# All twelve score products of a head pair ahead of its six masked minima, in a windowed attention with softplus FFN

## The chip, the core and the metric

The kernel runs on one core of one Trainium2 chip. The metric is the device time of one execution in microseconds (us). Five engines work beside each other, each with a queue of its own: TensorE (PE, with its weight loads shown as PEld), VectorE (DVE), ScalarE (ACT), GpSimd (POOL) and SyncE (SP, which issues the DMAs).

## The reference

A causal attention over a window of 64 positions, for 8 batches of 8 heads, sequences of 576 and a head size of 64, and behind it a dense layer pair with a softplus between them, on 4608 tokens of 512 numbers.

```
scores = scale * np.matmul(q, k.transpose(0, 1, 3, 2))
rel = pos[:, None] - pos[None, :]
mask = (rel >= 0) & (rel < window)
scores = np.where(mask, scores, -1000000000.0)
scores = scores - np.max(scores, axis=-1, keepdims=True)
attn = np.exp(scores)
attn = attn / (np.sum(attn, axis=-1, keepdims=True) + 1e-09)
x = np.matmul(attn, v)          # then (batch, position) x (head, channel)
h = x @ w_in
g = np.maximum(h, 0.0) + np.log1p(np.exp(-np.abs(h)))
out = g @ w_out
```

## The kernel before

**Tiles.** The 4608 tokens are cut into 12 blocks g of 384 tokens. A block's attention is done by head pairs hp (4 of them, two heads of 64 channels each), its FFN by 16 slices f of 128 hidden channels. So there are 48 head pairs and 192 FFN steps in all.

**Attention of one head pair** (`attention`, a generator whose `yield`s mark stages). The 384 query tokens are three query tiles j of 128, each of two chunks u of 64. A chunk needs the 128 keys of its own and the previous chunk. So a product of q and k (L219) is 64 queries by 128 keys, for one chunk and one head hh: twelve products per head pair, four per query tile. They are written to `sps`, one PSUM bank per head, in which the three query tiles stand beside each other in columns. VectorE's `tensor_tensor_reduce` (L226) then adds the mask to one query tile of one head, writes the scaled result to `st` and its minimum over the keys to `mn` (the scale is negative, so the minimum stands for the maximum). There are six of these per head pair. ScalarE takes six exponentials (L236), with the sums in `sm`; VectorE adds, inverts and multiplies (L244 to L246). For blocks 0 and 1 (`by_pe`) TensorE transposes the result (L254) and ScalarE copies it (L255); for the others it is split in two fp16 halves (ScalarE's cast `nat` L265, VectorE's rest L268), which DMAs transpose (L262) and VectorE adds (`pt`, L272). TensorE multiplies with v (L286), and the result is split into two parts x (ScalarE L291, VectorE L292), the FFN's input.

**FFN step** (g, f): `ffn_up` is twelve matmuls of 128x384 (L308) into one of two banks `ps_h`; ScalarE takes Abs, Exp and Ln (L312 to L314), VectorE completes softplus (L316), and g is split in two parts (L318 on ScalarE or VectorE, L319 on VectorE). `ffn_down` is nine matmuls of 128x512 (L329) into three banks `ps_o`; at a block's end they are copied (L348) and stored.

**Banks.** Scores and products with v take turns on three banks (`ps_a`, `bufs=3`). In block 0, odd head pairs use `ps_o` banks.

**What sets the order.** Every stage and FFN step is an event with a due time, two units of time per FFN step; events are sorted by it and emitted in that order. Up number n is due at 2n + 0.5 and down number n at 2n + 5.5, so a down comes three ups after its up has begun. From block 3 on, head pairs follow each other every 8 units (four FFN steps), and a head pair's stages are due at the offsets of `STG`: the loads at -13 and -5, the scores with their minima at 0, the exponentials at 3 and 4, the product with v at 16. That is when the scores of the head pair two further on are due, so in PE's queue L286 of one head pair stands directly in front of the scores of another. TensorE executes its work in exactly the emitted order (`MANUAL`); the other engines' order is made by a scheduler when the program is built. Each engine takes its own queue in order. The weights come as 64-bit words and are converted at the start (`load_w`: ScalarE L162 and L168, VectorE L163 to L165 and L169), beside the attention of blocks 0 and 1; their raw words share buffers with `st` of block 0.

Of the kernel before, what the change touches and what calls it, by code (L numbers as in the profile page):

```python
# [15 lines left out]
ALU = mybir.AluOpType  # L16

P = 128
TB = 384
NJ = TB // P  # L20
WIN = 64
BIG = 1.0e9
CH = 64
# [20 lines left out]
def window_attention_softplus_ffn(  # L44
# [34 lines left out]
    QSCALE = -1.0 / float(D) ** 0.5  # L79
# [22 lines left out]
    def spare(k, shape, dtype, name):  # L102
        return late.tile(shape, dtype, name=name, tag=f"spare{k}")
# [11 lines left out]
    heads = [slice(0, D), slice(D, P)]  # L115
    halves = [slice(0, CH), slice(CH, P)]
# [23 lines left out]
    mm, tp = nc.tensor.matmul, nc.tensor.transpose  # L140
# [34 lines left out]
    def attention(g, hp):  # L175
# [5 lines left out]
        def bank():  # L181
            if not odd0:
                return ps_a.tile([P, 512], F32, name="ps_a")

            taken_ps[0] += 1
            return ps_o.tile([P, 512], F32, name=f"ps_o{taken_ps[0] % NJ}")

        q_in = ld.tile([P, TB], F32, name="q_in", bufs=2)
        k_in = ld.tile([P, CH + TB], F32, name="k_in", bufs=2)
# [16 lines left out]
        if g == 0:  # L206

            st = spare(FIRST[hp], [P, 2, NJ, P], F32, "st0")
        else:
            st = att.tile([P, 2, NJ, P], F32, name="st", bufs=2)  # L210
        mn = att.tile([P, 2, NJ], F32, name="mn", bufs=2)
        sm = att.tile([P, 2 * NJ], F32, name="sm", bufs=2)
        sps = [bank() for _ in heads]
        for j in range(NJ):
            js = slice(j * P, (j + 1) * P)
            for u in range(2):
                a = 2 * j + u
                for hh in range(2):
                    mm(  # L219
                        sps[hh][halves[u], js], q_in[heads[hh], a * CH : (a + 1) * CH],  # L220
                        k_in[heads[hh], a * CH : (a + 2) * CH], start=True, stop=True,
                    )
            t = (t0 + j * P) % S
            m = mask_at[0] if t == 0 else mask_at[1] if t + P > S else mask
            for hh in range(2):
                nc.vector.tensor_tensor_reduce(  # L226
                    st[:, hh, j, :], sps[hh][:, js], m, QSCALE, 3.0e38, ALU.add, ALU.min, mn[:, hh, j : j + 1]
                )
            if by_pe or j == NJ - 1:
                yield  # L230
# [53 lines left out]
        for a, hh in itertools.product(range(2 * NJ), range(2)):  # L284
# [3 lines left out]
                start=(a == 0), stop=(a == 2 * NJ - 1), skip_group_check=True,  # L288
# [73 lines left out]
    for g in range(NB):  # L362
        for hp in range(NP):
            if g < 3:
                base = BASE[g] + PACE[g] * hp
            else:
                base = 2 * NF * (g - 1) + SHP * hp + SH
            stages = attention(g, hp)
            for at in STG if g >= 2 else STG0:
                events.append((base + at, lambda stages=stages: next(stages, None)))  # L370
# [59 lines left out]
```

## Time and profile before

| | |
|---|---|
| median of 3 runs | 1131.58 us (1131.5 to 1132.87) |
| profiled execution | 1132.96 us |
| span of its trace | 1131.2 us |
| mean granted TensorE clock | 0.957 |
| HBM traffic over the span | 59 GB/s |

The granted clock is the share of full speed that the chip's throttle gave TensorE. Its rows by stage are in the prediction. From about 100 us on, the kernel repeats one pattern: four FFN steps, then a product with v and the scores of a head pair. From 255 to 1010 us every such period has its scores; behind that none are left to do, and from 1047 us on only FFN steps. A matmul's record includes its way through the array, so records of queued matmuls overlap.

### The profile page before, as it was taken

How to read it: one execution, taken by the hardware profiler on the slowest of the kernel's cores; microseconds unless marked ns; L12 is line 12 of the kernel's file. 1: busy time of each engine (PE TensorE's matmuls, PEld its weight loads, DVE VectorE, ACT ScalarE, POOL GpSimd, SP SyncE). 2: the span in 40 equal slices, each digit the busy share in tenths (PEclk: the TensorE clock that was granted, in tenths of full speed). 3: DMA queues.
4: the chain of work that ended last, by engine and by line, in shares of the span. 5: the costliest groups of instructions: out<-in, count | busy, mean ns of one | idle time of the engine just before them, and what ended most of it. 6: DMA issues, size and time to landing. Idle time of an engine off the chain costs nothing.

```text
span 1131.2 us, 16632 instructions
## 1 busy us (share of the span) xinstructions
PE 1006.9 (89%) x6384; PEld 864.2 (76%) x6384; DVE 552.5 (49%) x1431; ACT 579.7 (51%) x1433; POOL 3.9 (0%) x23
## 2 busy tenths in 40 slices
PE   5449899998999899989998999899989999899998
PEld 3338787887887788878887788778877787788997
DVE  5895754545444444444445444544444544543332
ACT  5665666554445444455445544555455544544443
POOL 1000000000000000000000000000000000000000
PEclk9989999999999999998999999999998999999999
DMA  7652522312223223123112221222222311320000
GB/s 233 245 170 98 159 59 79 107 44 86 60 57 72 57 60 85 44 57 92 53 43 69 79 55 44 83 62 57 72 54 62 86 44 43 86 43 1 28 1 28
DMA packets 124048, 83.65 MB, mean 74 GB/s; under 512 B 67137, under 2 KB 116033, under 8 KB 122433
## 3 DMA queue, kind: packets, MB, share of 16 engines
q1 hardware_dynamic: 123968, 82.60, 25.5%
q8 instruction: 50, 0.82, 0.3%
q14 instruction: 30, 0.24, 0.1%
HBM read 56.62 MB, written 10.22 MB: 59 GB/s over the span
## 4 chain that ended last, share of the span: by engine, by line
PE 80%; DVE 11%; DMA 5%; ACT 2%; issue 1%; POOL 0%; POOLq 0%; ACTq 0%; SPq 0%; DVEq 0%
PE ps_h L308 38%; PE ps_o L329 34%; PE ps_a L219 5%; DMA raws<-in_w_words_dram 4%; PE ps_a L286 3%; DVE pt L272 3%; DVE st L226 2%; DVE g L319 2%; DVE x L292 1%; DMA raw<-in_w_words_dram 1%; ACT ws L162 1%; DVE w L169 0%; DVE ws L165 0%; DVE ws L164 0%; ACT st L236 0%
## 5 line engine op out<-in xcount | busy, mean ns | idle before, releaser
L308 PE MATMUL ps_h<-x,w 128*128 128x384 f32 x2304 | 476.0, 359 | 0.0
L308 PEld LDWEIGHTS ps_h<-x,w 128*128 128x128 f32 x2304 | 439.5, 203 | 20.8 <-issue 7.3
L329 PE MATMUL ps_o<-w,g 128*128 128x512 f32 x1728 | 437.0, 397 | 0.0
L329 PEld LDWEIGHTS ps_o<-w,g 128*128 128x128 f32 x1728 | 326.8, 191 | 61.4 <-DVE g L319 0.4
L316 DVE SCALAR_TENSOR_TENSOR u<-ps_h,u 128x384 f32<-128x384 f32 x192 | 106.9, 557 | 332.1 <-ACT u L314 332.1
L312 ACT ACTIVATE u<-ps_h 128x384 f32<-128x384 f32 x192 | 94.3, 491 | 312.7 <-PE ps_h L308 311.9
L219 PE MATMUL ps_a<-k_in,q_in 64*64 64x128 f32 x1104 | 93.3, 315 | 106.1 <-DVE mn L226 102.3
L219 PEld LDWEIGHTS ps_a<-k_in,q_in 64*64 64x64 f32 x1104 | 47.6, 140 | 144.2 <-DVE mn L226 134.5
L236 ACT ACTIVATE st<-st,mn 128x128 f32<-128x128 f32 x288 | 113.6, 395 | 74.5 <-DVE mn L226 74.3
L319 DVE TENSOR_TENSOR g<-u,g 128x384 fp32r<-128x384 f32 x192 | 106.9, 557 | 41.3 <-ACT g L318 35.5
L313 ACT ACTIVATE u<-u 128x384 f32<-128x384 f32 x192 | 100.9, 526 | 5.8
L314 ACT ACTIVATE u<-u 128x384 f32<-128x384 f32 x192 | 100.7, 525 | 5.4
L226 DVE CUSTOM_DVE_ANT_0 st<-ps_a,mask 128x128 f32<-128x128 f32 x276 | 71.3, 286 | 49.7 <-PE ps_a L219 49.4
L318 ACT CAST g<-u 128x384 fp32r<-128x384 f32 x112 | 57.3, 512 | 59.0 <-DVE u L316 57.7
L268 DVE TENSOR_TENSOR nat<-st,nat 128x768 f16<-128x768 f32 x40 | 38.3, 958 | 51.0 <-ACT nat L265 51.0
L286 PEld LDWEIGHTS ps_a<-pt,v_in 128*64 128x64 f32 x1104 | 38.9, 143 | 21.6 <-issue 15.9
L236 ACT ACTIVATION_READ_ACCUMULATOR st<-st,mn 128x1 f32 x288 | 53.8, 187 | 0.0
L265 ACT CAST nat<-st 128x768 f16<-128x768 f32 x40 | 33.1, 827 | 40.5 <-issue 40.5
L286 PE MATMUL ps_a<-pt,v_in 128*64 128x64 f32 x1104 | 46.0, 232 | 4.6 <-ACT pt L255 3.8
L272 DVE TENSOR_TENSOR pt<-tr 128x768 f32<-128x768 f16 x40 | 38.3, 958 | 23.0 <-PE ps_a L286 21.7
L246 DVE TENSOR_TENSOR st<-st,sm 128x768 f32<-128x768 f32 x48 | 46.0, 958 | 1.5
L318 DVE CAST g<-u 128x384 fp32r<-128x384 f32 x80 | 28.8, 360 | 5.7
(48 smaller groups left out, 277.2 us busy)
## 6 DMA issues: line engine op xcount, KB each, us to landing
v_in<-in_v_dram SPq DMA_DIRECT2D x44, 384.0 KB, 3.4
raws<-in_w_words_dram SPq DMA_DIRECT2D x12, 1024.0 KB, 5.6
k_in<-in_kT_dram SPq DMA_DIRECT2D x44, 224.0 KB, 2.7
q_in<-in_qT_dram SPq DMA_DIRECT2D x48, 192.0 KB, 2.4
out_dram<-raw SPq DMA_DIRECT2D x12, 512.0 KB, 3.0
raw<-in_w_words_dram SPq DMA_DIRECT2D x8, 512.0 KB, 3.7
out_dram<-raw SPq DMA_DIRECT2D x12, 256.0 KB, 4.1
v_in<-in_v_dram SPq DMA_DIRECT2D x4, 320.0 KB, 4.2
```

Of the source, the lines that this page charges most:

```text
L219: mm(sps[hh][halves[u], js], q_in[heads[hh], a * CH : (a + 1) * CH], k_in[heads[hh], a * CH : (a + 2) * CH], start=True, stop=True,)
L226: nc.vector.tensor_tensor_reduce(st[:, hh, j, :], sps[hh][:, js], m, QSCALE, 3.0e38, ALU.add, ALU.min, mn[:, hh, j : j + 1])
L236: nc.scalar.activation(sv[:, i, :], sv[:, i, :], AF.Exp, bias=mn[:, hh, j : j + 1], scale=-1.0, accum_out=sm[:, i : i + 1])
L286: mm(av[heads[hh], cs], v_in[:, a, heads[hh]], pt[:, hh, cs], start=(a == 0), stop=(a == 2 * NJ - 1), skip_group_check=True,)
L308: mm(hv, weight(0, a, f)[:, c * P : (c + 1) * P], x[b][c], start=(i_mm == 0), stop=(i_mm == 3 * NC - 1))
L312: nc.scalar.activation(u, hv, AF.Abs)
L313: nc.scalar.activation(u, u, AF.Exp, scale=-1.0)
L314: nc.scalar.activation(u, u, AF.Ln, bias=1.0)
L316: nc.vector.scalar_tensor_tensor(gf, hv, 0.0, u, ALU.max, ALU.add)
L318: (nc.scalar.copy if g < 2 or f % 2 else nc.vector.tensor_copy)(gt[0], gf)
L319: nc.vector.tensor_tensor(gt[1], gf, gt[0].bitcast(F32), ALU.subtract)
L329: mm(ops[g][j], gt[a][:, js], weight(1, b, f), start=(first and i == 0), stop=(last and i == 2),)
```

## The change

The four products of a query tile stood directly ahead of its two minima, tile by tile. Now one loop emits all twelve products, in the order as before (tile, chunk, head), and a second loop the six minima, also in the order as before. The stages' ends (`yield`) stand with the minima as before. Lines behind this place have numbers smaller by one in the changed kernel: L216 is the product there, L224 the minimum, L307 and L328 the FFN's matmuls.

```
+        for j, u, hh in itertools.product(range(NJ), range(2), range(2)):
+            a = 2 * j + u
+            mm(
+                sps[hh][halves[u], j * P : (j + 1) * P], q_in[heads[hh], a * CH : (a + 1) * CH],
+                k_in[heads[hh], a * CH : (a + 2) * CH], start=True, stop=True,
+            )
         for j in range(NJ):
-            js = slice(j * P, (j + 1) * P)
-            for u in range(2):
-                a = 2 * j + u
-                for hh in range(2):
-                    mm(
-                        sps[hh][halves[u], js], q_in[heads[hh], a * CH : (a + 1) * CH],
-                        k_in[heads[hh], a * CH : (a + 2) * CH], start=True, stop=True,
-                    )
             t = (t0 + j * P) % S
             m = mask_at[0] if t == 0 else mask_at[1] if t + P > S else mask
             for hh in range(2):
                 nc.vector.tensor_tensor_reduce(
-                    st[:, hh, j, :], sps[hh][:, js], m, QSCALE, 3.0e38, ALU.add, ALU.min, mn[:, hh, j : j + 1]
+                    st[:, hh, j, :], sps[hh][:, j * P : (j + 1) * P], m,
+                    QSCALE, 3.0e38, ALU.add, ALU.min, mn[:, hh, j : j + 1],
                 )
             if by_pe or j == NJ - 1:
                 yield
```

PE's queue has the same instructions in the same order. What differs there are the semaphores that they wait for. Before, at one head pair late in the steady stage (ps_a are the score banks, ps_h the next FFN step's; xN is the number of equal rows):

```order
L286 MATMUL ps_a<-pt,v_in 64x64 [waits DMAHW0_49,PE_49]
L286 MATMUL ps_a<-pt,v_in 64x64 x11
L219 MATMUL ps_a<-k_in,q_in 64x128 [waits DMAHW2_49,DMAHW1_49,PE_49]
L219 MATMUL ps_a<-k_in,q_in 64x128 [waits PE_49]
L219 MATMUL ps_a<-k_in,q_in 64x128 x2
L219 MATMUL ps_a<-k_in,q_in 64x128 [waits DVE_49] x2
L219 MATMUL ps_a<-k_in,q_in 64x128 x2
L219 MATMUL ps_a<-k_in,q_in 64x128 [waits DVE_49] x2
L219 MATMUL ps_a<-k_in,q_in 64x128 x2
L308 MATMUL ps_h<-x_0_0_6837,w_85 128x384
```

And the same place in the changed program:

```order
L285 MATMUL ps_a<-pt,v_in 64x64 [waits DMAHW0_49,PE_49]
L285 MATMUL ps_a<-pt,v_in 64x64 x11
L216 MATMUL ps_a<-k_in,q_in 64x128 [waits DMAHW2_49,DMAHW1_49,PE_49]
L216 MATMUL ps_a<-k_in,q_in 64x128 [waits PE_49]
L216 MATMUL ps_a<-k_in,q_in 64x128 x10
L307 MATMUL ps_h<-x_0_0_6837,w_85 128x384 [waits DVE_49]
```

The four products that waited for VectorE, two at the second and two at the third query tile, wait for nothing now; the FFN's first matmul behind them carries a wait for VectorE that the products had covered.

ScalarE's queue around the exponentials of one steady head pair, before:

```order
L291 ACTIVATE x_0_1_4563<-ps_a 128x384
L236 ACTIVATE st,sm<-st,mn 128x128 x6
L265 CAST nat<-st 128x768
L312 ACTIVATE u<-ps_h 128x384
L313 ACTIVATE u<-u 128x384
L314 ACTIVATE u<-u 128x384
```

And in the changed program:

```order
L290 ACTIVATE x_0_1_4563<-ps_a 128x384
L235 ACTIVATE st,sm<-st,mn 128x128 x6
L311 ACTIVATE u<-ps_h 128x384
L312 ACTIVATE u<-u 128x384
L313 ACTIVATE u<-u 128x384
L264 CAST nat<-st 128x768
```

The cast `nat` moved behind the three functions of the next FFN step. On VectorE, the same head pair's rows before:

```order
L272 TENSOR_TENSOR pt<-tr 128x768
L319 TENSOR_TENSOR g_4542<-u,g_4541 128x384
L226 ISA st,mn<-ps_a,mask_103 128x128
L226 ISA mn 128x1
L292 SCALAR_TENSOR_TENSOR x_0_1_4564<-ps_a,x_0_1_4563 128x384
L226 ISA st,mn<-ps_a,mask_103 128x128
```

And in the changed program:

```order
L271 TENSOR_TENSOR pt<-tr 128x768
L318 TENSOR_TENSOR g_4542<-u,g_4541 128x384
L291 SCALAR_TENSOR_TENSOR x_0_1_4564<-ps_a,x_0_1_4563 128x384
L224 ISA st,mn<-ps_a,mask_103 128x128
L224 ISA mn 128x1
L224 ISA st,mn<-ps_a,mask_103 128x128
```

The second part of x moved ahead of the first minimum; further down, the rest of `nat` (L268) moved from ahead of the next L316 to behind it and the cast of g (L318). In the first 100 us, conversions and minima change places on VectorE and ScalarE in many rows, and on SP's queue some loads of raw weights stand elsewhere among the loads of k and v. SP's queue is otherwise the same, but for one load of `part`.

## The prediction

> **What bounds the kernel now.** I read the page first (busy time by engine), then the waits, then TensorE's timeline around one head pair, then windows from one head pair to the next.
>
> ```profile
> PE 1006.9 (89%) x6384; PEld 864.2 (76%) x6384; DVE 552.5 (49%) x1431; ACT 579.7 (51%) x1433; POOL 3.9 (0%) x23
> ```
>
> ```profile
> PE ps_a L219 <- DVE mn L226: 102.3, 125, 4.7
> ```
>
> TensorE (PE) is busy 1006.9 of 1131.2 us; VectorE (DVE) and ScalarE (ACT) about half. Nearly all that PE lacks is one wait, 102.3 us: score products (L219) waiting for masked minima (L226). What it looks like, in rows of PE's timeline (start, duration, engine, line, operation, count, idle time before):
>
> ```profile
> 981.72 0.92 PE L286 MATMUL ps_a<-pt,v_in 128*64 128x64 f32 x24
> 982.57 0.45 PE L219 MATMUL ps_a<-k_in,q_in 64*64 64x128 f32 x8
> 984.38 0.43 PE L219 MATMUL ps_a<-k_in,q_in 64*64 64x128 f32 x2 [1.36 <-DVE mn L226]
> 985.05 0.44 PE L219 MATMUL ps_a<-k_in,q_in 64*64 64x128 f32 x6 [0.25 <-DVE mn L226]
> 985.89 0.65 PE L219 MATMUL ps_a<-k_in,q_in 64*64 64x128 f32 x8 [0.40 <-DVE mn L226]
> 986.48 3.91 PE L308 MATMUL ps_h<-x,w 128*128 128x384 f32 x12
> 990.23 2.26 PE L329 MATMUL ps_o<-w,g 128*128 128x512 f32 x9
> ...
> 142.84 4.16 PE L308 MATMUL ps_h<-x,w 128*128 128x384 f32 x12
> ...
> 1029.17 2.37 PE L308 MATMUL ps_h<-x,w 128*128 128x384 f32 x12
> ```
>
> Twelve products show as 24 records, eight for each query tile. From 982.57 to 986.48 they hold PE for 3.91 us, most of it waiting twice for minima of the tile before: both tiles stand in one PSUM bank. Then twelve L308 matmuls hold PE 3.75 us (986.48 to 990.23). Windows from one L286 to the next (length, busy time by engine; the number after POOL is PE's granted clock):
>
> ```profile
> 959.99:981.72 21.73, 19.73 (x133) 16.88 (x132) 10.93 (x30) 11.54 (x29) 0.00 (x0) 1.00 0.30 57
> 981.72:1005.03 23.31, 21.31 (x133) 18.45 (x132) 10.85 (x30) 11.35 (x29) 0.00 (x0) 0.93 0.28 68
> 1028.32:1046.12 17.80, 17.80 (x109) 15.88 (x108) 6.51 (x13) 7.69 (x15) 0.00 (x0) 1.00 0.00 1
> ...
> 254.55:1028.32 773.77, 705.82 (x4489) 608.13 (x4488) 358.54 (x971) 383.81 (x960) 0.00 (x0) 0.95 0.23 62
> ```
>
> The third window holds the same four FFN steps and the same L286, but no scores: 17.80 us with PE never idle. With scores it is 21.73 at clock 1.00, or 23.31 at 0.93: **the waits cost twice**, as idle time and, in many periods, as a slow clock behind them. The last row is the whole steady stage: 4488 weight loads at 132 a period are 34 periods. At 21.73 each they would take 738.8; the 35.0 us left over are about 22 periods of the slow kind (1.58 each).
>
> **The change part by part.** It adds and removes no instruction. PE's order is the same; what goes are the two waits inside each head pair's scores. The six minima wait for the last product of their bank, so nothing on PE stands between a head pair's first score and the L308 behind it.
>
> *Price of the scores alone.* The first eight above take 0.45 with a last matmul of about 0.27, so they start 0.18 apart, and the next eight could start at 0.21: three times that is 0.63. Below, the weight load of L308 shows a changeover.
>
> ```profile
> 508.68 3.56 PEld L308 LDWEIGHTS ps_h<-x,w 128*128 128x128 f32 x12 [0.17 <-issue]
> ```
>
> 0.63 + 0.17 = 0.80, my value: the scores stay queued behind L286 as the first eight are. The lower bound is 0.63; the upper is three times what the last eight take after a wait, 986.48 - 985.89 = 0.59, so 1.77.
>
> *Steady stage.* 34 x (17.80 + 0.80) = 632.4 in place of 773.77: **-141.4**, of which about 35 is clock.
>
> *The six head pairs before it* have no L286 beside their scores (first, second and the sum of six windows from first score to next step):
>
> ```profile
> 136.17:142.84 6.67, 1.95 (x26) 1.11 (x25) 6.34 (x18) 4.77 (x13) 0.00 (x0) 0.79 0.48 151
> 159.47:161.96 2.49, 1.69 (x25) 0.98 (x24) 1.14 (x9) 2.35 (x8) 0.00 (x0) 1.00 0.01 3
> sum 19.11, PE 10.38 PEld 6.04 DVE 13.74 ACT 15.44 POOL 0.00; mean PE 1.73 PEld 1.01 DVE 2.29 ACT 2.57 POOL 0.00
> ```
>
> 19.11 becomes 6 x 0.80 = 4.8: **-14.3**. The first is also followed by a slow L308 (4.16 in the timeline above, against 2.37 at 1029.17, where the clock is 1.00): **-1.8**.
>
> *The head, 0 to 100 us*, with eight head pairs and the weight conversion:
>
> ```profile
> 0.00:28.00 28.00, 15.64 (x148) 10.50 (x148) 14.76 (x60) 15.58 (x52) 3.94 (x23) 1.00 0.73 233
> 28.00:56.00 28.00, 13.32 (x118) 9.09 (x119) 24.38 (x57) 17.85 (x47) 0.00 (x0) 1.00 0.71 249
> 56.00:84.00 28.00, 13.59 (x121) 10.00 (x120) 27.27 (x59) 18.48 (x48) 0.00 (x0) 0.90 0.52 173
> 84.00:100.00 16.00, 14.26 (x100) 11.89 (x102) 9.80 (x20) 9.64 (x22) 0.00 (x0) 0.85 0.37 118
> ```
>
> Here DVE is the bound from 28 to 84 (51.65 of 56), so PE's waits there are mostly hidden: PE would only wait elsewhere. DVE's idle time from 28 to 100 is 10.6 us, the most there is to win. The scheduler also reorders conversions and minima here, and SP's loads of raws move past loads of v_in; the two dearest kinds of a conversion's DVE steps are
>
> ```profile
> L169 DVE TENSOR_TENSOR w<-ws,w 128x512 fp32r<-128x512 f32 x24 | 15.7, 681 | 0.3 <-ACT w L168 0.3
> L164 DVE SCALAR_TENSOR_TENSOR ws<-raws,ws 128x1024 uint32<-128x1024 uint32 x12 | 14.7, 1222 | 0.1
> ```
>
> two of each, some 3.8 us; two such conversions ahead of minima that end the head would cost 7.6. I take **-4**, between +7.6 and -10.6, nearer the gain, because PE's waits there hold back the transposes and products behind them, which ScalarE and DVE go on from.
>
> *What the moved DVE and ACT work does.* In the steady stage x (L292) goes ahead of the first minimum, and ACT's nat cast (L265) and DVE's L268 go behind the next u. Is anything late for PE's next steps? One period in order, with durations from rows (L313 taken as L314, L319 and x as L316, L246 and L268 as L272, which has as many elements):
>
> ```profile
> 504.89 0.96 DVE L272 TENSOR_TENSOR pt<-tr 128x768 f32<-128x768 f16 x1 [0.75 <-PE ps_a L286]
> ...
> 507.96 0.28 DVE L226 CUSTOM_DVE_ANT_0 st<-ps_a,mask 128x128 f32<-128x128 f32 x1
> 508.17 0.08 DVE L226 DVE_READ_ACCUMULATOR2_ANT mn<- 128x1 f32 x1
> ...
> L316 DVE SCALAR_TENSOR_TENSOR u<-ps_h,u 128x384 f32<-128x384 f32 x192 | 106.9, 557 | 332.1 <-ACT u L314 332.1
> L312 ACT ACTIVATE u<-ps_h 128x384 f32<-128x384 f32 x192 | 94.3, 491 | 312.7 <-PE ps_h L308 311.9
> L236 ACT ACTIVATE st<-st,mn 128x128 f32<-128x128 f32 x288 | 113.6, 395 | 74.5 <-DVE mn L226 74.3
> L314 ACT ACTIVATE u<-u 128x384 f32<-128x384 f32 x192 | 100.7, 525 | 5.4
> L265 ACT CAST nat<-st 128x768 f16<-128x768 f32 x40 | 33.1, 827 | 40.5 <-issue 40.5
> ```
>
> Let L286 start at 0. PE: scores 0.85 to 1.65, L308 to 3.9, L329 to 5.95, next L308 to 8.05, L329 to 10.15, third L308 from 10.15; it needs the first one's bank, and the L329 at 12.25 needs its g. DVE: pt 0.96 to 1.9, L319 to 2.4, x to 2.9, six minima at 0.21 (507.96 to 508.17) to 4.15. ACT: six exponentials from 3.2, 0.40 each, to 5.6, then L312 to L314, 1.6, to 7.2. DVE: L246 to 7.1, L316 to 7.75 (bank free, due 10.15), the cast to 8.1, L268 after ACT's nat (8.05) to 9.05, L319 to 9.6 (due 12.25). So the cover is 2.4 us: **0**, and each us beyond it would cost 34. The loads of a period (first window) of 11.5 (ACT) and 10.9 (DVE) fit in 18.6.
>
> **Sum.** The profiled execution took 1132.96 us (1.38 over the median, 1131.58): 1132.96 - 141.4 - 14.3 - 1.8 - 4 = **971.5**.
>
> **Rivals.**
>
> *The clock stays slow.* If the thin matmuls (L286 and scores, 1.65 us at a stretch) and not the idle time bring the clock down, the 35 us stay: 1006. For it: the pattern of fast and slow periods depends on where the stretch falls. Against: the 2.49 us window at 159.47, scores with idle time in it, ran at 1.00, as did L286 alone at 1028.32. The Trainium skill ("TensorE: Matmul & The Clock Gate", "Why this matters for your kernels") says that only idle gaps over about 3 us throttle the array. By that rule the slow L308 would have another cause, and the sum would be this rival's. The trace speaks against the rule: no gap here is over 1.36, yet L308 took 3.91.
>
> *The products come at the slow pace*, 1.77: 40 x 0.97 = 38.8 more, 1010. For it: pace after a wait. Against: no wait is left before them.
>
> *DVE and ACT become late* by 1 us beyond the 2.4 in each period: 1005; by 2, 1040. For it: in-order queues with a burst of exponentials. Against: the replay above.
>
> *Nothing happens*: a wait for minima stays for another reason, 1131. Against: PE's rows of the change hold none.
>
> *Slower*: PE without pauses is held to a lower clock in the steady stage. It decides below 971.5/1132.96 = 0.86; at 0.79, the lowest row above, 971.5/0.79 = 1230. Against:
>
> ```profile
> 100.00:136.00 36.00, 36.00 (x190) 32.62 (x186) 21.18 (x39) 22.27 (x45) 0.00 (x0) 1.00 0.38 122
> 1028.00:1131.00 103.00, 98.79 (x530) 88.28 (x528) 34.16 (x64) 42.12 (x82) 0.00 (x0) 0.99 0.04 16
> ```
>
> PE was busy 36.00 of 36 and 98.79 of 103 us at clocks of 1.00 and 0.99. The Trainium skill (same page, Part 1) has a limiter at 13/16 clock once three cores of a die run dense matmuls; one runs here, and no run here shows it.
>
> **How the numbers follow.** Forecast 0.80, clock stays slow 0.08, late engines 0.05, slow pace 0.03, nothing 0.02, slower 0.02. Anything beyond 0.2% of 1131.58, about 2.3 us, can be told from no change. Faster 0.96, same 0.02, slower 0.02. The range: down by the rest of the head (6.6) and of the scores (40 x 0.17 = 6.8) to 958; up to the slow pace, 1010, which takes in the clock's rival and the first us of the late engines.
>
> **What would show it.** Right: L219 without a wait for L226, 0.7 to 1 us from first score to next step, periods of 18.6, granted clock near 1.00 from 255 us on, the end of the head within 10 us of 100. Wrong: L308 groups of 3.7 us still behind scores (clock), PE waiting for L316 or L319 (late engines), or the head longer by more than 7.6.

## Result and profile after

The changed kernel takes **969.12 us** (median of 4 runs, 967.93 to 974.21) where the kernel before takes 1132.22 us beside it (4 runs, 1131.5 to 1133.0): a ratio of 0.857, 95% interval 0.854 to 0.860. The forecast was 971.5 us. The profiled execution is the slowest of the four, 974.21 us with a span of 972.4; the working below goes by it. In the changed kernel the scores are L216, the minima L224 (two lower than before), and the lines behind them one lower: L286 has become L285, and the two FFN products are L307 and L328.

The page's busy times and granted clock in 40 slices:

```profile
PE 923.3 (95%) x6384; PEld 814.9 (84%) x6384; DVE 539.0 (55%) x1431; ACT 564.5 (58%) x1433; POOL 3.9 (0%) x23
...
PEclk9568989999999999999999999999999999999999
```

The number of instructions on each engine is the same. TensorE's busy time fell by 83.6 us (1006.9 to 923.3) although it does the same matmuls. The larger part are the records of the products themselves, which overlap less when products wait in between:

```profile
L219 PE MATMUL ps_a<-k_in,q_in 64*64 64x128 f32 x1104 | 93.3, 315 | 106.1 <-DVE mn L226 102.3
...
L216 PE MATMUL ps_a<-k_in,q_in 64*64 64x128 f32 x1104 | 44.8, 297 | 3.8 <-DMA k_in<-in_kT_dram 3.8
```

These are 48.5 us. The FFN's matmuls, slow ones before among them, fell from 476.0 to 443.8 and from 437.0 to 433.5. The granted clock is at 90% or more from the seventh slice on. It is lower in the second to fourth slices, which lie in the head, and in the sixth (122 to 146 us). TensorE's waits, the longest first, have no row for scores that wait for minima, where before had 102.3 us in it. The first row, a wait in the head for ScalarE's copies of the transposed results, has grown from 3.8 us to 11.3:

```profile
PE ps_a L285 <- ACT pt L254: 11.3, 9, 3.7
...
PE ps_h L307 <- DVE u L315: 3.4, 1, 3.4
```

The timeline at one head pair of the steady stage (start, duration, line, operation, count), and at the one place behind the head where a new wait stands:

```profile
254.79 0.92 PE L285 MATMUL ps_a<-pt,v_in 128*64 128x64 f32 x24
255.64 0.89 PE L216 MATMUL ps_a<-k_in,q_in 64*64 64x128 f32 x24
256.45 2.38 PE L307 MATMUL ps_h<-x,w 128*128 128x384 f32 x12
258.67 2.26 PE L328 MATMUL ps_o<-w,g 128*128 128x512 f32 x9
...
140.36 4.21 PE L307 MATMUL ps_h<-x,w 128*128 128x384 f32 x12 [3.36 <-DVE u L315]
144.37 3.00 PE L328 MATMUL ps_o<-w,g 128*128 128x512 f32 x9
```

The twelve products are now one group of 24 records that hold TensorE for 0.81 us (255.64 to 256.45) where they held it for 3.91 at 982.57 before, and the L307 behind them takes 2.38 us, not the 3.91 of that place. At 140.36, once, the third L307 waits for VectorE and then runs slowly. Windows (length, busy time by engine, clock) over the head, one period, the whole steady stage and the period without scores:

```profile
0.00:28.00 28.00, 13.98 (x162) 11.01 (x162) 14.23 (x54) 14.28 (x47) 3.94 (x23) 0.85 0.75 238
28.00:56.00 28.00, 10.72 (x110) 8.04 (x110) 24.75 (x68) 19.57 (x57) 0.00 (x0) 0.50 0.75 260
...
236.12:254.79 18.67, 18.67 (x133) 16.56 (x133) 10.74 (x31) 10.69 (x28) 0.00 (x0) 1.00 0.36 109
236.12:869.59 633.47, 633.47 (x4490) 561.61 (x4489) 347.25 (x971) 370.77 (x960) 0.00 (x0) 1.00 0.29 76
869.59:887.38 17.79, 17.79 (x109) 15.87 (x108) 6.50 (x13) 7.69 (x15) 0.00 (x0) 1.00 0.00 1
```

In the steady stage TensorE is busy 633.47 of 633.47 us at clock 1.00; before, the same 34 periods took 773.77. By line, over these two windows, the difference of 140.3 is about 68 us of idle time in front of products, 37 in the products' own records (67.1 to 30.1) and 36 in the FFN's matmuls (344.8 to 311.5 and 309.2 to 306.6), which is the part of the slow clock. By stages, before against after:

| stage | before, us | after, us | difference | predicted |
|---|---|---|---|---|
| head, to the first two L307 groups in a row | 100.20 | 91.53 | -8.7 | -4 |
| from there to the steady stage, six head pairs | 154.35 | 144.59 | -9.8 | -16.1 |
| steady stage, 34 periods | 773.77 | 633.47 | -140.3 | -141.4 |
| sum, with the rest of the span (equal within 0.1) | | | -158.8 | -161.5 |

### The profile page after: what moved, and what is told of

It is laid out like the page before. It is cut to its first block, busy times and chain, and to the rows that moved or that the text cites. A ratio compares the mean times of both kernels' runs of the same rounds, so it can differ in the third digit from the quotient of the medians.

```text
span 972.4 us, 16615 instructions
## 1 busy us (share of the span) xinstructions
PE 923.3 (95%) x6384; PEld 814.9 (84%) x6384; DVE 539.0 (55%) x1431; ACT 564.5 (58%) x1433; POOL 3.9 (0%) x23
## 4 chain that ended last, share of the span: by engine, by line
PE 87%; DMA 6%; DVE 3%; ACT 3%; issue 0%; SPq 0%; ACTq 0%; DVEq 0%
PE ps_h L307 41%; PE ps_o L328 39%; PE ps_a L285 4%; DMA raws<-in_w_words_dram 4%; PE ps_a L216 3%; DMA raw<-in_w_words_dram 2%; ACT st L235 1%; ACT ws L162 1%; DVE w L169 1%; DVE ws L164 0%; DVE ws L165 0%; DMA part<-raw 0%; DVE st L245 0%; ACT wh L162 0%; DVE st L224 0%
## 5 line engine op out<-in xcount | busy, mean ns | idle before, releaser
L307 PE MATMUL ps_h<-x,w 128*128 128x384 f32 x2304 | 443.8, 341 | 3.4 <-DVE u L315 3.4
L328 PE MATMUL ps_o<-w,g 128*128 128x512 f32 x1728 | 433.5, 395 | 1.4 <-DVE g L318 1.4
L307 PEld LDWEIGHTS ps_h<-x,w 128*128 128x128 f32 x2304 | 409.1, 189 | 24.1 <-issue 6.9
L328 PEld LDWEIGHTS ps_o<-w,g 128*128 128x128 f32 x1728 | 322.2, 188 | 62.3 <-DVE g L318 2.0
L315 DVE SCALAR_TENSOR_TENSOR u<-ps_h,u 128x384 f32<-128x384 f32 x192 | 107.0, 557 | 253.4 <-ACT u L313 249.7
L235 ACT ACTIVATE st<-st,mn 128x128 f32<-128x128 f32 x288 | 111.9, 391 | 67.1 <-DVE mn L224 67.1
L318 DVE TENSOR_TENSOR g<-u,g 128x384 fp32r<-128x384 f32 x192 | 106.6, 555 | 38.7 <-ACT g L317 33.8
L312 ACT ACTIVATE u<-u 128x384 f32<-128x384 f32 x192 | 100.9, 526 | 5.8
L317 ACT CAST g<-u 128x384 fp32r<-128x384 f32 x112 | 57.4, 512 | 57.7 <-DVE u L315 56.6
L285 PEld LDWEIGHTS ps_a<-pt,v_in 128*64 128x64 f32 x1104 | 40.1, 146 | 34.1 <-issue 20.2
L224 DVE CUSTOM_DVE_ANT_0 st<-ps_a,mask 128x128 f32<-128x128 f32 x276 | 61.8, 286 | 9.6 <-PE ps_a L216 9.6
L285 PE MATMUL ps_a<-pt,v_in 128*64 128x64 f32 x1104 | 47.6, 236 | 16.8 <-ACT pt L254 11.3
L216 PE MATMUL ps_a<-k_in,q_in 64*64 64x128 f32 x1104 | 44.8, 297 | 3.8 <-DMA k_in<-in_kT_dram 3.8
L216 PEld LDWEIGHTS ps_a<-k_in,q_in 64*64 64x64 f32 x1104 | 32.7, 144 | 8.6 <-POOL mask L135 3.8
L243 DVE TENSOR_SCALAR sm<-sm 128x6 f32<-128x6 f32 x40 | 6.9, 172 | 54.4 <-ACT st L235 54.3
```

The source lines that it names most:

```text
L216: mm(sps[hh][halves[u], j * P : (j + 1) * P], q_in[heads[hh], a * CH : (a + 1) * CH], k_in[heads[hh], a * CH : (a + 2) * CH], start=True, ...
L224: nc.vector.tensor_tensor_reduce(st[:, hh, j, :], sps[hh][:, j * P : (j + 1) * P], m, QSCALE, 3.0e38, ALU.add, ALU.min, mn[:, hh, j : j + 1],)
L235: nc.scalar.activation(sv[:, i, :], sv[:, i, :], AF.Exp, bias=mn[:, hh, j : j + 1], scale=-1.0, accum_out=sm[:, i : i + 1])
L285: mm(av[heads[hh], cs], v_in[:, a, heads[hh]], pt[:, hh, cs], start=(a == 0), stop=(a == 2 * NJ - 1), skip_group_check=True,)
L307: mm(hv, weight(0, a, f)[:, c * P : (c + 1) * P], x[b][c], start=(i_mm == 0), stop=(i_mm == 3 * NC - 1))
L312: nc.scalar.activation(u, u, AF.Exp, scale=-1.0)
```

## The experiments

Seven new kernels, and the changed kernel once more. Each stands beside runs of the kernel before on its own chip (1131.7 to 1132.3 us). Theory A is the prediction's: the waits between the products cost their idle time and, through the clock, slow matmuls behind them. Its main rival was that the thin matmuls, and not the idle time, bring the clock down.

### Half of the change: steady stage alone, and head alone

A helper emits the four products of one tile, either all ahead or tile by tile; `by_pe` is true in blocks 0 and 1, the head. This is the edit for the steady stage alone; for the head alone the line reads `ahead = NJ if by_pe else 0`.

```diff
-        for j, u, hh in itertools.product(range(NJ), range(2), range(2)):
+        def products(j):
...
+        ahead = 0 if by_pe else NJ
+        for j in range(ahead):
+            products(j)
         for j in range(NJ):
...
+            if j >= ahead:
+                products(j)
```

Steady stage alone (blocks 2 and later):

> The change for blocks 2 to 11 alone (40 head pairs), blocks 0 and 1 as before. My theory: the terms are separate, so this keeps the steady stage (34 periods of 18.63 in place of 22.76, about 140 us) and the six head pairs ahead of it, and loses only the head's gain (8.7 us in the trace of the change: 100.20 against 91.53): 974 to 980 us, granted clock 1.00 in the steady stage. Rival: the head's gain is chance or comes back later as waits for weights: 967 to 971.

Head alone:

> The change for blocks 0 and 1 alone (8 head pairs), the 40 others as before. My theory: PE's waits in the head held back transposes and products, so the end of the head moves from 100.2 to about 91.5 us: 1121 to 1126 us. Rival: the head is bound by DVE and by the loads of weights, and nothing is won there: 1130 to 1133.

Measured: **980.07 us** for the steady stage alone (979.52 to 980.74, 4 runs; ratio 0.866, interval 0.864 to 0.867) and **1121.31 us** for the head alone (1117.56 to 1122.76, 4 runs; ratio 0.990, interval 0.987 to 0.992). The second lies in theory A's range, the first at its upper edge, 0.07 us beyond it and far from the rival's. So the change in the head is worth 10.9 us by the one (980.07 - 969.12; 8.9 against 971.16, the second set of runs of the changed kernel, further down) and 10.9 by the other (1132.16 - 1121.31), more than the 4 of the forecast, and the two halves add up within 2 us.

Where does the head's gain come from? VectorE is the bound there, and it loses both idle time and work. The sums of four windows over the head, first of before and then of after, and VectorE's rows of one step of the large weight conversions inside each head:

```profile
sum 100.20, PE 57.02 PEld 41.61 DVE 76.41 ACT 61.56 POOL 3.94; mean PE 14.25 PEld 10.40 DVE 19.10 ACT 15.39 POOL 0.98
L164 DVE SCALAR_TENSOR_TENSOR ws<-raws,ws 128x1024 uint32<-128x1024 uint32 x12 | 14.7, 1222 | 0.1
```

```profile
L164 DVE SCALAR_TENSOR_TENSOR ws<-raws,ws 128x1024 uint32<-128x1024 uint32 x11 | 13.4, 1222 | 0.1
```

Before, VectorE was busy 76.41 of 100.20 us of the head, idle 23.8. In the first 91.50 us of after it is busy 70.22 (14.23 + 24.75 above, and 22.32 + 8.92 in two more windows up to 91.50), idle 21.3. Of the 8.7 us, 2.5 are idle time that went and 6.2 are busy time. Most of that, 4.5, is one of the twelve large conversions, which now comes later (x12, x11): two steps of 1.22 us, two of 0.68 and one of 0.69. Another 0.6 is one step of the FFN that comes later too, and 1.2 are the minima: the same 48, whose records overlap more when they follow each other directly (12.0 to 10.8). Behind the head VectorE has slack for the conversion: it is busy 87.67 of the 144.59 us up to the steady stage. The prediction named the reordered conversions only as a risk.

The profiled execution of after is the slowest of its four, and its head is longer than in two other traces of the changed head. With the head alone and with the changed kernel again, the head ends at 89.49 and 88.40 us, and VectorE is idle for 18.4 and 17.4 us of it. So there 5.4 and 6.4 of the 10.7 and 11.8 us are idle time that went, about half.

In both kernels that change blocks 2 and later there is also the new wait. With the steady stage alone, where the head is as before, TensorE's timeline has it too (its lines are L314 for L307 and L322 for L315):

```profile
148.22 2.03 PE L314 MATMUL ps_h<-x,w 128*128 128x384 f32 x10 [3.15 <-DVE u L322]
```

So the wait does not come from the conversion that was put off in the head. (The row ends with its window, at 150 us. The whole group takes 2.38 us: behind this wait of 3.15 us nothing is slow.)

### What brings the clock down: thin matmuls five times over, without a gap

```diff
-        for j, u, hh in itertools.product(range(NJ), range(2), range(2)):
+        for _, j, u, hh in itertools.product(range(1 if by_pe else 5), range(NJ), range(2), range(2)):
```

> The change, with the twelve products of each head pair in blocks 2 to 11 made five times over (same results): PE has small matmuls for as long a stretch as before, about 4 us, and no idle time in it. Forty head pairs with 4 x 0.65 to 0.81 us more are 104 to 130 us. If idle time brings the clock down: 1073 to 1100 us at a granted clock of 1.00 in the steady stage. If the small matmuls do: about 35 us more, 1108 to 1135, and L307 groups of 3.7 us behind two periods in three.

Measured: **1076.12 us** (2 runs). The timeline of a steady period:

```profile
418.48 0.92 PE L285 MATMUL ps_a<-pt,v_in 128*64 128x64 f32 x24
419.32 3.51 PE L216 MATMUL ps_a<-k_in,q_in 64*64 64x128 f32 x120
422.76 2.37 PE L307 MATMUL ps_h<-x,w 128*128 128x384 f32 x12
```

4.28 us of thin matmuls at a stretch (418.48 to 422.76), and the L307 behind them takes 2.37 us, the full pace. The products cost 3.44 instead of 0.81; 40 times the difference is 105 us, and 969.12 + 105 = 1074. Between 250 and 960 us the granted clock is 1.00. The rival falls: thin matmuls without a gap do not bring the clock down.

### One gap in each period

One product is emitted again behind the six minima, into columns that the last of them read, so TensorE waits for them:

```diff
+            if not by_pe and j == NJ - 1:
+                mm(
+                    sps[1][halves[1], j * P : (j + 1) * P], q_in[heads[1], 5 * CH : 6 * CH],
+                    k_in[heads[1], 5 * CH : 7 * CH], start=True, stop=True,
+                )
```

> The change, with one more product (a repeat of the last one, same result) behind the six minima in blocks 2 to 11: it waits for the minima of its bank, so PE has a single idle gap of about 2.5 us per steady period, with the small matmuls ahead of it. The gap and the product are 34 x 2.9 + 6 x 1.7 = 109 us. If idle time of this size brings the clock down as before: 22 to 34 periods x 1.58 = 35 to 54 us more, 1113 to 1132 us, granted clock about 0.95 in the steady stage. If only gaps over some 3 us do: about 1078 us at a clock of 1.00.

Measured: **1117.01 us** (1113.48 to 1120.54, 2 runs). Two periods of the timeline, the first slow, the second fast (L312 is the L307 of after, L333 its L328):

```profile
521.32 0.43 PE L229 MATMUL ps_a<-k_in,q_in 64*64 64x128 f32 x2 [2.44 <-DVE mn L224]
521.68 3.37 PE L312 MATMUL ps_h<-x,w 128*128 128x384 f32 x12
524.85 2.86 PE L333 MATMUL ps_o<-w,g 128*128 128x512 f32 x9
...
544.79 2.38 PE L312 MATMUL ps_h<-x,w 128*128 128x384 f32 x12
```

A single gap of 2.44 us is enough for slow matmuls behind it, though not in every period: the granted clock is 0.92 from 519 to 541 us and 1.00 from 541 to 563. The time lies in the range for a clock that falls. By the row of the Trainium skill that the prediction weighed ("TensorE: Matmul & The Clock Gate", "Why this matters for your kernels"), idle gaps over about 3 us are the ones to avoid; here the trace disagrees.

All these gaps stand behind thin matmuls. Behind the head, a gap between FFN matmuls stands at one place only, the new wait that ends between 137 and 149 us. Four traces have it: 3.15 us long in the steady stage alone, 3.21 in the changed kernel again, 3.36 in after and 3.50 with the thin matmuls five times over. Slow matmuls follow the last three (L307 groups of 4.21, 4.21 and 3.33 us), but not the first. A gap of 2.4 us between FFN matmuls alone is not tested.

### One of the two waits left

Blocks 2 and later emit tile 0, its minima, and then tiles 1 and 2 with theirs, with the helper from above:

```diff
+        if by_pe:
+            for j in range(NJ):
+                products(j)
+        else:
+            products(0)
         for j in range(NJ):
+            if not by_pe and j == 1:
+                products(1)
+                products(2)
```

> In blocks 2 and later one wait is left of the two: the products of tile 0, its minima, and then tiles 1 and 2 with theirs. From the rows of before, tile 1 starts 1.81 us behind tile 0 (984.38 - 982.57) and may wait once more for 0.25 us; the scores would hold TensorE for 2.6 to 3.3 us in place of 0.81. Over 40 head pairs that is 72 to 100 us: 1041 to 1071 us if gaps of 1.4 us leave the clock alone. If they bring it down as in before, where two gaps stood in each period, the slow periods cost some 35 us on top: 1076 to 1106 us, with L307 groups of 3.4 to 3.9 us behind the scores.

Measured: **1061.5 us** (2 runs, 1061.49 and 1061.52; ratio 0.938, interval 0.936 to 0.941). The timeline of one of the slow periods (L317 is the L307 of after, L338 its L328):

```profile
448.81 0.43 PE L217 MATMUL ps_a<-k_in,q_in 64*64 64x128 f32 x2 [1.36 <-DVE mn L234]
449.48 0.66 PE L217 MATMUL ps_a<-k_in,q_in 64*64 64x128 f32 x14 [0.25 <-DVE mn L234]
450.07 3.48 PE L317 MATMUL ps_h<-x,w 128*128 128x384 f32 x12
453.36 2.71 PE L338 MATMUL ps_o<-w,g 128*128 128x512 f32 x9
```

The time falls into the range for a clock left alone, but the timeline shows that this isn't quite so: some periods are slow. From 450.07 to 472.49 us the granted clock is 0.92, in the period before it 1.00. I counted in the timelines between 230 and 1030 us how many L307 groups straight behind scores take over 2.7 us (2.35 to 2.39 is the full pace):

| kernel | idle time of TensorE in the scores of a steady period, us | slow groups |
|---|---|---|
| before | 1.36 + 0.25 + 0.40 = 2.01 | 23 of 35 |
| one gap | 2.44 | 19 of 35 |
| one wait left | 1.36 + 0.25 = 1.61 | 8 of 34 |
| after | 0 | 0 of 34 |
| thin five times | 0 | 0 of 35 |

So gaps decide it, and 1.61 us of them already does now and then. No single threshold on their length fits: 2.01 us in three pieces is slow more often than 2.44 in one. What picks the slow periods stays open.

### The order of before, with FFN work between the tiles

Each tile's four products and two minima are a stage of their own, so that a piece of FFN work stands between them:

```diff
-STG = (-13, -5, 0, 3, 4, 5, 6, 7, 13, 16)
+STG = (-13, -5, 0, 1, 2, 3, 4, 5, 6, 7, 13, 16)
...
-            if by_pe or j == NJ - 1:
-                yield
+            yield
```

> The order of before (one query tile's four products, then its two minima, then the next tile), but for blocks 2 and later each tile is a stage of its own, so that a piece of feed-forward work of some 2 us stands on TensorE between one tile and the next. If what the change removed is TensorE's idle time and its slow clock, and not the order in which the banks are used, the minima of a tile run beside the feed-forward piece and the waits go: about 975 to 990 us (the head as before, 9 us more than after the change; three changeovers instead of one, 0.3 to 0.5 us per period more on 34 periods). If the order by tiles itself costs the time, the waits of TensorE for VectorE's minima stay: 1100 us or more.

Measured: **1004.4 us** (2 runs, 1004.0 and 1004.79; ratio 0.887, interval 0.885 to 0.889). Neither range holds it, but the mechanism is the first: the waits in the steady stage are gone, and no L307 there is slow. My price for the changeovers was too low. The timeline of one period:

```profile
532.66 0.92 PE L285 MATMUL ps_a<-pt,v_in 128*64 128x64 f32 x24
533.51 0.45 PE L219 MATMUL ps_a<-k_in,q_in 64*64 64x128 f32 x8
533.89 2.35 PE L307 MATMUL ps_h<-x,w 128*128 128x384 f32 x12
536.17 0.45 PE L219 MATMUL ps_a<-k_in,q_in 64*64 64x128 f32 x8
536.55 2.33 PE L328 MATMUL ps_o<-w,g 128*128 128x512 f32 x9
538.82 0.45 PE L219 MATMUL ps_a<-k_in,q_in 64*64 64x128 f32 x8
539.20 2.35 PE L307 MATMUL ps_h<-x,w 128*128 128x384 f32 x12
541.38 2.25 PE L328 MATMUL ps_o<-w,g 128*128 128x512 f32 x9
543.47 2.28 PE L307 MATMUL ps_h<-x,w 128*128 128x384 f32 x12
...
551.96 0.92 PE L285 MATMUL ps_a<-pt,v_in 128*64 128x64 f32 x24
```

The period is 19.30 us (551.96 - 532.66), against 18.67 in a window of after. The products take 3 x 0.38 = 1.14 instead of 0.81, and two of the FFN pieces take 2.28 and 2.27 from start to start where one with no scores on either side takes 2.09 (541.38 to 543.47). That is 0.33 + 0.37 = 0.70 a period, or 28 us over 40 head pairs. The mean of 33 periods (242.55 to 880.77 us) agrees: 19.34 against 18.63 in after. With the head as before the mark is the steady stage alone, 980.07 + 28 = 1008. Its wait of 3.15 us for VectorE is not in the trace of this kernel, which makes 1005, close to 1004.4. The grouped order beats this one because it changes over once.

### The new wait: block 2 later

A second theory concerns the shortfall between head and steady stage. The stages of block 2 come three units later, and a unit closer together:

```diff
-BASE = (-80, -40, 24)
-PACE = (10, 10, 7)
+BASE = (-80, -40, 27)
+PACE = (10, 10, 6)
```

> The changed kernel with the stages of block 2 put three units later and a unit closer together, so that its first head pair comes after the conversion of the weights. If the 3.36 us wait of the third product group L307 at 140 us, and the slow clock behind it, come from VectorE and ScalarE having the conversion to do at that place, the wait goes and 5 to 7 us with it: 962 to 965 us. If the two engines are late there for another reason, or the work that is put off is missed later, the wait stands at another place: 967 to 971 us.

The changed kernel again on the same chip:

> The changed kernel once more on the same chip, as the mark for the run with block 2 later: 967 to 971 us by either theory.

Measured: **966.12 us** (965.38 to 966.87, 4 runs) against **971.16** (970.24 to 971.32, 5 runs) for the changed kernel there: 5.0 us less, the intervals against before being 0.852 to 0.855 and 0.856 to 0.859. That is the lower end of the 5 to 7 expected (the time itself is 1.1 us above the range). In the two profiled executions the head ends at 90.31 and 88.40 us, so behind the head the spans differ by 6.3 us. The timeline of block 2's first head pair:

```profile
132.66 0.89 PE L216 MATMUL ps_a<-k_in,q_in 64*64 64x128 f32 x24
133.48 2.36 PE L328 MATMUL ps_o<-w,g 128*128 128x512 f32 x9
135.67 2.26 PE L307 MATMUL ps_h<-x,w 128*128 128x384 f32 x12
```

No wait follows and no slow matmul. In after, VectorE's and ScalarE's queues at that place read, in rows of their timelines (start, duration, engine, line, operation):

```profile
129.03 0.69 DVE L165 SCALAR_TENSOR_TENSOR wh<-raw,wh 128x512 uint32<-128x512 uint32 x1
...
132.62 0.28 DVE L224 CUSTOM_DVE_ANT_0 st<-ps_a,mask 128x128 f32<-128x128 f32 x1
...
139.15 0.68 DVE L169 TENSOR_TENSOR w<-wh,w 128x512 fp32r<-128x512 f32 x1
139.75 0.55 DVE L315 SCALAR_TENSOR_TENSOR u<-ps_h,u 128x384 f32<-128x384 f32 x1
```

```profile
132.94 0.40 ACT L235 ACTIVATE st<-st,mn 128x128 f32<-128x128 f32 x1 [1.16 <-DVE mn L224]
...
137.32 0.52 ACT L312 ACTIVATE u<-u 128x384 f32<-128x384 f32 x1
138.25 0.52 ACT L313 ACTIVATE u<-u 128x384 f32<-128x384 f32 x1
```

The products were done at 128.34 (they start at 127.53 there), but the first minimum starts at 132.62, behind conversion steps such as L165; ScalarE's exponentials begin at 132.94, the L312 that the FFN needs at 137.32, and VectorE's L315, which frees the bank, at 139.75. The third L307 needs that bank. Before the change the same L307 group had no such wait: TensorE was itself held by the scores for 6.67 us there. With block 2 later, the last conversion step of VectorE (138.05) comes 5.4 us behind the first product of block 2; in after it is 11.6 (139.15 - 127.53). That moving the head pair away from the conversion removes the wait fits the theory. The kernel with FFN work between the tiles also fits: it has the same conversion beside this head pair, its minima come two at a time, and TensorE has no such wait. The move of block 2 also shifts its later head pairs and puts these scores ahead of an L328 instead of an L307, so it is no proof that the conversion alone delays the two engines.

## Why the prediction was right, step by step

- **What bounds the kernel** was right: the waits cost twice. The idle part and the slow part went together, and the experiments with thin matmuls, one gap and one wait show that gaps bring the slow part, and thin work without gaps does not. The FFN's matmuls gave back 36 us of the steady stage, for 35 in the forecast. Which gaps do it stays open.
- **The price of the scores** was right: 0.81 us measured, 0.80 predicted. The rival with the slow pace, 1.77, did not occur.
- **The steady stage** was right: -140.3 against -141.4. The period is 18.63 us (633.47 / 34), 18.60 was predicted. The rival of the clock that stays slow (1006) fell; its clock is 1.00.
- **Late VectorE and ScalarE**: 0 in every steady period, as worked out. In the period from 254.79 us VectorE frees the bank 7.60 us after L285's start (7.75 in the replay), and the third L307 starts at 10.18: the cover is 2.6 us, for 2.4. But the replay was made of a steady period only. In the first head pair of block 2, where the weight conversion still runs on both engines, the 2.4 us of cover were not there. This is the rival of the late engines, at one place: 3.36 us of waiting, and behind it 1.84 (L307, 4.21 against 2.37) and 0.74 (L328, 3.00 against 2.26) for the slow clock, 5.9 us of the 6.3 by which the step "six head pairs" fell short.
- **The head** had the right sign and the wrong size: -8.7 in the trace of after, -10.7 and -11.8 in two others, 10.9 by the medians, for -4. The bound of 10.6 taken from VectorE's idle time was not the right kind of bound, since 5.3 to 6.2 us are busy time that left the head, most of it one large conversion. The conversions that I feared ahead of the minima went the other way. Their price was also misread: L164 stands in a conversion once, beside an L165 of the same size, and with L163 it is 4.5 us, not 3.8.
- **The sum** hit because the errors nearly cancel: of the gain, the forecast had 4.7 us too little in the head, 6.3 too much behind it, 1.1 too much in the steady stage. By the terms they are 2.7 us for the profiled execution, 974.2 for 971.5; the median, 969.1, is 2.4 on the other side. That the steady stage fits is no luck, since its parts fit one by one; that the rest adds up to so little is.

## What to carry to other kernels

When an engine waits several times inside a short step, look at what runs behind the step too: here a quarter of the steady gain (36 of 140 us) was slow matmuls after the gaps, which no row of waits shows. Emitting all producers ahead of their consumers removes the gaps where the banks allow it, and here it is cheaper than hiding each gap behind other work, which cost 0.7 us more per period in changeovers. But the consumers then arrive at their engines as one packet, so replay the replaced queue where those engines have most else to do, and not in the steady period alone.

## What the runs showed of the hardware that was not expected

- TensorE's clock fell after a single gap of 2.44 us behind small matmuls in 19 of 35 periods, and after gaps of 1.36 + 0.25 us in 8 of 34; a slow L307 group takes 3.1 to 3.9 us instead of 2.37. It did not fall after 4.28 us of small matmuls without a gap, nor after one gap of 3.15 us between FFN matmuls.
- In the head of the changed kernel the granted clock was 0.50 from 28 to 56 us, where before had 1.00, and yet the head became shorter: VectorE was busy 24.75 of those 28 us, TensorE 10.72.
- A group of eight score records between two FFN pieces costs 0.38 us plus some 0.18 us on the FFN piece that stands before the next group (2.27 against 2.09), where the same eight cost 0.27 in a queue of 24.
